# Value weights loaded first, and the last tokens' values of seven blocks computed in the start of a recurrent-memory transformer layer

## The chip, the cores and the metric

The kernel runs on one core of a Trainium2 chip. A core has five engines with queues of their own, each taking its instructions in the order in which they were written: PE (matrix products), DVE (vector), ACT (scalar functions and copies), POOL (general) and SP, which here only starts transfers. The metric is the device time of one execution in microseconds (us). Before the change it is 1035.0 us, the median of three runs (1034.61 to 1038.56).

## The reference

A layer with a recurrent memory over 2048 tokens of width 640, then a dense layer. The tokens are cut into 64 segments of 32. Each segment is preceded by eight memory tokens, and the memory of the next segment is the output of the attention at those eight places. So segment s+1 can't start before segment s has its memory.

```python
mem = mem0                                             # 8 x 640
for s in range(n_seg):                                 # 64 segments
    xs = x[:, s * seg_len:(s + 1) * seg_len, :]        # 32 tokens, normalised
    h = jnp.concatenate([mem, xs], axis=1)             # 40 rows
    q, k, v = h @ Wq, h @ Wk, h @ Wv                   # 32 heads of 128 each
    scores = jnp.where(mask, q @ k.T * scale, -1e9)    # all see mem, tokens causal
    o = softmax(scores) @ v
    o = einsum('bhte,hed->btd', o, Wo)
    mem = o[:, :M, :]
    outs.append(o[:, M:, :])
h = x + concatenate(outs)
h2 = h + relu(layernorm(h) @ w1 + b1) ** 2 @ w2 + b2
```

## The kernel before

**Tiling.** Sixteen blocks of four segments; a segment is one step, written (b, sp). Of the 40 rows of a segment, 32 (8 of memory and the first 24 tokens) are projected in the step itself, with four matrix products side by side in the four 32-column strips of PE (`proj`). The last 8 tokens of the four segments of a block, 32 rows together, are projected apart, since they need no memory: `tail_units(b, which)` gives ten units of four matmuls for q, k or v of block b. A unit is small work that can be put anywhere; the list `fill` holds the units waiting, and `run(fill, n)` in a step issues n of them at places where PE would wait: one before the values, two after them, five while the output is summed, the rest while the memory is transposed.

**What a block's fill is.** In block b (from 1 to 14), step sp=0 carries the ten value units of block b+1, sp=1 its q units, sp=2 its k units, and sp=3 ten units of the output product of the last tokens of block b-1. In block 0 all thirty units of block 1 run in step (0,0), and (0,1) to (0,3) carry none.

**Values through DRAM.** The values of the last tokens are wanted in another arrangement than the projection gives. `tail_out` copies a half (n = 0 or 1) into a row buffer (four in rotation, shared with the q and k rows of the steps), `tails_v` writes it to DRAM (`vt_d`, two blocks in rotation) and `tails_v_in` reads it back into `vt4`. Flips of q and k rows, statistics and sums that are to run at the head of a step are put into the list `late`; `mid` and `win` are lists for the norm and the transposes of a coming block.

**The start.** ACT starts the loads of x blocks 0 and 1 and of the first memory, SP the four weight matrices in the order wq, wk, wv, wo (5.2 MB each). `ln_stats`, `ln_norm` and `ln_transpose` prepare a block of 128 rows: statistics on DVE, two small operations on POOL (L151, L152), the norm on DVE, five transposes on PE, and two copies on ACT, one to `hT4` (first 24 tokens of each segment, L180) and one to `hTt` (last 8, L181). `start()` then projects segment 0 and the last tokens of block 0 chunk by chunk, as the weights come: q, k, v. After it, `tails_in` brings the q and k of the last tokens to their place (POOL), and step (0,0) begins with scores. In this step POOL issues the four reads of block 0's values.

**Semaphores of transfers.** Transfers started by SP and ACT share eight semaphores in turn, and a transfer is started only once the one before it on the same semaphore has landed.

Of the kernel before, what the change touches and what calls it, by code (L numbers as in the profile page):

```python
# [9 lines left out]
ALU = mybir.AluOpType  # L10
# [6 lines left out]
def kernel(  # L17
# [16 lines left out]
    nc = tc.nc  # L34
# [83 lines left out]
    def load_x(b, eng=nc.sync):  # L118
        xt = s2.tile([128, D], BF16, tag="xt", name="xt")
        eng.dma_start(out=xt[:], in_=x2d[b * 128:(b + 1) * 128, :])  # L120
        xts[b] = xt

    load_x(0, nc.scalar)
    load_x(1, nc.scalar)
    o_ring = [const.tile([128, DH], BF16, name="o%d" % k) for k in range(5)]
    for o in o_ring:
        nc.gpsimd.memset(o[64:128], 0.0)
# [2 lines left out]
    for ch in range(2):  # L130
        nc.scalar.dma_start(out=o0[32 * ch:32 * ch + M, :].rearrange("m (c f) -> m c f", f=64),
                            in_=A_mem0[0].rearrange("m (c t f) -> t m c f", t=2, f=64)[ch])
    load_w(wq, A_Wq)
    load_w(wk, A_Wk)
    load_w(wv, A_Wv)
    wov = A_Wo.rearrange("h e d -> e h d")
    for n in range(2):
        for j in range(2):
# [30 lines left out]
    def ln_transpose(b):  # L169

        xn = xns.pop(b)
        pt = mm.tile([128, 1024], BF16, tag="mm", name="pt")
        for c in range(DC):
            nc.tensor.transpose(out=pt[:, c * 128:(c + 1) * 128], in_=xn[:, c * 128:(c + 1) * 128], identity=ident[:])

        def out():
            hT4 = s2.tile([128, DC, 4, SEG], BF16, tag="hT4", name="hT4")
            hTt = s2.tile([128, DC, TL, 4], BF16, tag="hTt", name="hTt")
            ptv = pt[:, 0:640].rearrange("p (c s t) -> p c s t", c=DC, s=4)
            nc.scalar.copy(out=hT4[:, :, :, M:SEG], in_=ptv[:, :, :, 0:HD])  # L180
            nc.scalar.copy(out=hTt[:].rearrange("p c k s -> p c s k"), in_=ptv[:, :, :, HD:SEG])  # L181
            hT4s[b], hTts[b] = hT4, hTt
        return out

    def proj(w, by, lhs, n, ps, c0, c1):
# [20 lines left out]
    def rowtile():  # L206
        return s2.tile([128, 512], BF16, tag="row", name="row", bufs=4)

    def evac_row(which, row, ps):
        if which == "q":  # L210
            nc.scalar.mul(out=row[:], in_=ps, mul=scale)  # L211
        else:
            nc.scalar.copy(out=row[:], in_=ps)  # L213

    def flip(row, dst, n):
        nc.vector.transpose(out=dst[:, n * 16:(n + 1) * 16, 0:32], in_=row[:].rearrange("p (h e) -> p h e", e=32))  # L216

    wov2 = wo[:].rearrange("p h (c t f) -> p h t c f", t=2, f=64)

# [10 lines left out]
    def wo_out(pw):  # L230
        o = o_ring[0]
        o_ring.append(o_ring.pop(0))
        tmp = s1.tile([64, DH], F32, tag="otmp", name="otmp")
        nc.scalar.copy(out=tmp[:], in_=pw[64:128, 0:DH])  # L234
        nc.vector.tensor_tensor(out=o[0:64], in0=pw[0:64, 0:DH], in1=tmp[:], op=ALU.add)  # L235
        return o

    fill, late, mid, win = [], [], [], []
# [1 line left out]
    def run(q, n):  # L240
        while n > 0 and q:
            q.pop(0)()
            n -= 1

    def tail_units(b, which):
        w = {"q": wq, "k": wk, "v": wv}[which]
        lhs = lambda c: hTts[b][:, c].rearrange("p k s -> p (k s)")
# [12 lines left out]
    def tail_out(b, which, n, ps):  # L260
        row = rowtile()
        evac_row(which, row, ps)
        if which == "v":
            tails_v(b, n, row)
            return
        if n == 0:
            tails.setdefault(b, {})[which] = s2.tile([128, H, 32], BF16, tag=which + "Tt", name=which + "Tt")
        dst = tails[b][which]
        late.append(lambda: flip(row, dst, n))
# [32 lines left out]
                              in_=k.unsqueeze(2).to_broadcast([128, H, 4, TL]))  # L302

    vt4s = {}
    vt_d = dram.tile([2, 4, 128, 2 * E], BF16)

    def tails_v(b, n, row):

        eng = nc.scalar if b < 2 else nc.sync
        eng.dma_start(out=vt_d[b % 2, 2 * n:2 * n + 2].rearrange("j r f -> r j f"),  # L310
                      in_=row[:].rearrange("r (j f) -> r j f", j=2))
        if n == 0:
            return
        vt4s[b] = s2.tile([128, 4, 2, E], BF16, tag="vt4", name="vt4")
        if b:
            tails_v_in(b, nc.sync)

    def tails_v_in(b, eng):
        src = vt_d[b % 2].rearrange("j (g k s) f -> g j k (s f)", g=G, s=4)
        for g in range(G):  # L320
            eng.dma_start(out=vt4s[b][32 * g:32 * g + 32].rearrange("p s u e -> p (s u e)"), in_=src[g])

# [31 lines left out]
    def step(b, sp, v=None):  # L354
# [1 line left out]
        last = s == NS - 1  # L356
        hT4 = hT4s[b]
        lhs = lambda c: hT4[:, c, sp, :]
        vt4 = vt4s[b]
# [3 lines left out]
        run(late, 3)  # L363

        def project(which, w, dst, n, between=None):
            if ready:
                if between:
                    between()
                return
            ps = mmtile()  # L370
            proj(w, "columns", lhs, n, ps, 0, DC)
            row = rowtile()
            if not between:
                evac_row(which, row, ps[:])
                flip(row, dst, n)
# [214 lines left out]
    ck, cv = Carve(wk), Carve(wv)  # L590
    f1T = ck(FC * NT).rearrange("p (c t) -> p c t", c=FC)
    hnT0 = const.tile([128, DC, NT], BF16, name="hnT0")
    hnTs = [hnT0[:], ck(DC * NT).rearrange("p (c t) -> p c t", c=DC)]
    ht0 = [const.tile([128, D], BF16, name="ht0%d" % k) for k in range(NK4)]
    ots = [ck(D) for _ in range(4)]
    fxs = [ck(D) for _ in range(4)]
    hbs = [cv(D, F32) for _ in range(2 * NK4)]
# [48 lines left out]
    def start():  # L646

        v = s2.tile([128, EG], BF16, tag="v", name="v")
        tail = lambda c: hTts[0][:, c].rearrange("p k s -> p (k s)")
        main = lambda c: hT4s[0][:, c, 0, :]  # L650
        for which, w, dst in (("q", wq, qT), ("k", wk, kT), ("v", wv, None)):
            pa = pop.tile([128, 4, 512], F32, tag="po", name="pa")
            for c in range(DC):
                for n in range(2):
                    proj(w, "half" if which == "v" else "columns", main, n, pa[:, n, :], c, c + 1)
                for n in range(2):
                    proj(w, "order" if which == "v" else "columns", tail, n, pa[:, 2 + n, :], c, c + 1)
            for n in range(2):
                if which == "v":
                    nc.scalar.copy(out=v[:, n * 512:(n + 1) * 512], in_=pa[:, n, :])  # L660
                else:
                    row = rowtile()
# [7 lines left out]
    for b in range(2):  # L670
        ln_stats(b)
        ln_norm(b)
        ln_transpose(b)()
        if b == 0:
            mem_to_hT(o0, hT4s[0], 0)
    v0 = start()
    tails_in(0, 0)
    for b in range(NB):
        for sp in range(4):
            run(soon, 1)  # L680
            if sp == 0 and b + 2 < NB:
                load_x(b + 2)
            if b == 0 and sp == 0:
                fill += tail_units(1, "v") + tail_units(1, "q") + tail_units(1, "k")
            if 0 < b < NB - 1 and sp < 3:
                fill += tail_units(b + 1, "vqk"[sp])
            if sp == 3 and 0 < b < NB - 1:
                fill += wo_tail_units(b - 1)
            if b == NB - 1 and 0 < sp < 3:
# [5 lines left out]
                mid.append(lambda b=b: ln_norm(b + 2))  # L695
            if b + 2 < NB and sp == 3:
                win.append(lambda b=b: ln_transpose(b + 2))
            e = b * 4 + sp - (NS - 7)
            if (b, sp) == (1, 0):
                ffn_biases()  # L700
# [120 lines left out]
```

## Time and profile before

| | |
|---|---|
| median of the runs | 1035.0 us (1034.61 to 1038.56) |
| the profiled execution | 1033.77 us, its span 1032.0 us |
| PE busy | 974.3 us, 94% of the span |
| DVE, ACT, POOL busy | 618.4, 536.8, 309.0 us |
| step 1's first matmul | 67.0 us |
| steps (0,1) to (15,2) | 66.74 to 882.52 us |
| dense layer and end | the rest |
| mean granted PE clock | 0.992 |

The length of a step is read here from one copy of the memory into `hT` (L296) to the next. Over blocks 1 to 14 (105.84 to 841.94) a step takes 13.15 us on average; the shortest take 12.79. The steps with sp=0 of blocks 1 to 14 took 14.06, 13.16, 13.31, 13.13, 12.96, 13.27, 13.07, 12.89, 12.90, 13.04, 13.26, 12.89, 13.20 and 13.38 us.

A page of the profile lists the busy share of each engine in forty slices. The chain of waits follows the last instruction back, at each step to what released it. The timeline lists instructions in order of time, with the idle time before them and what ended it in brackets. A table of stretches gives the busy time of each engine between two times and the granted clock there.

### The profile page before, as it was taken

How to read it: one execution, taken by the hardware profiler on the slowest of the kernel's cores; microseconds unless marked ns; L12 is line 12 of the kernel's file. 1: busy time of each engine (PE TensorE's matmuls, PEld its weight loads, DVE VectorE, ACT ScalarE, POOL GpSimd, SP SyncE). 2: the span in 40 equal slices, each digit the busy share in tenths (PEclk: the TensorE clock that was granted, in tenths of full speed). 3: DMA queues.
4: the chain of work that ended last, by engine and by line, in shares of the span. 5: the costliest groups of instructions: out<-in, count | busy, mean ns of one | idle time of the engine just before them, and what ended most of it. 6: DMA issues, size and time to landing. Idle time of an engine off the chain costs nothing.

```text
span 1032.0 us, 59015 instructions
## 1 busy us (share of the span) xinstructions
PE 974.3 (94%) x26940; PEld 563.6 (55%) x26940; DVE 618.4 (60%) x1724; ACT 536.8 (52%) x1237; POOL 309.0 (30%) x797
## 2 busy tenths in 40 slices
PE   3678999999999999999999999999999998899998
PEld 1245555565556555555555556555556565555565
DVE  2145566666666666666666666666666676566532
ACT  2235555555555555555555555555555555534431
POOL 1023333333333333333323232333233333343210
PEclk9889999999999999999999999999999999999999
DMA  9930101010000000000000000000000110612200
GB/s 378 396 105 5 33 7 32 10 29 13 25 17 27 14 24 18 25 17 26 17 14 27 15 27 15 26 15 27 15 27 8 52 34 7 195 61 66 77 26 26
DMA packets 38538, 50.93 MB, mean 49 GB/s; under 512 B 6097, under 2 KB 34385, under 8 KB 36369
## 3 DMA queue, kind: packets, MB, share of 16 engines
q1 hardware_dynamic: 36496, 46.04, 13.5%
q8 instruction: 210, 3.44, 1.4%
q10 hardware_dynamic: 1472, 0.86, 0.3%
q0 software_dynamic: 320, 0.26, 0.1%
q14 instruction: 40, 0.32, 0.1%
HBM read 37.71 MB, written 9.44 MB: 46 GB/s over the span
## 4 chain that ended last, share of the span: by engine, by line
PE 86%; DMA 6%; DVE 3%; ACT 2%; issue 2%; SPq 0%; POOL 0%; ACTq 0%; DVEq 0%; POOLq 0%
PE ps L195 46%; PE pw L227 15%; PE y L772 6%; PE ps L740 5%; PE ps L227 3%; PE po L431 2%; DMA wv<-in_A_Wv_dram 2%; PE sm L403 2%; PE pm L294 2%; DMA vt_d<-row 1%; PE po L338 1%; DMA wk<-in_A_Wk_dram 1%; PE ps L477 1%; ACT em L412 1%; DMA xt<-in_A_x_dram 1%
## 5 line engine op out<-in xcount | busy, mean ns | idle before, releaser
L195 PEld LDWEIGHTS <-hT 128*32 128x32 bf16 x7680 | 187.7, 96 | 184.9 <-DVE hT L296 19.2
L195 PE MATMUL ps<-wv,hT 128*32 128x512 bf16 x2520 | 169.9, 379 | 0.7 <-ACT v L484 0.7
L227 PE MATMUL pw<-wo,oT 128*32 128x320 bf16 x4224 | 161.9, 302 | 5.0 <-issue 2.1
L195 PE MATMUL ps<-wq,hT 128*32 128x512 bf16 x2520 | 158.2, 380 | 2.4 <-DVE hT L296 2.4
L195 PE MATMUL ps<-wk,hT 128*32 128x512 bf16 x2520 | 157.7, 379 | 0.0
L227 PEld LDWEIGHTS <-oT 128*32 128x32 bf16 x4224 | 110.4, 97 | 53.2 <-DVE oT L202 16.5
L527 POOL TENSOR_TENSOR pkt<-ek,rk 128x64 bf16<-128x64 bf16 x64 | 19.0, 296 | 374.5 <-DVE rk L525 293.8
L211 ACT ACTIVATE row<-ps 128x512 bf16<-128x512 f32 x156 | 91.9, 600 | 73.1 <-PE ps L195 69.6
L216 DVE STREAM_TRANSPOSE qT<-row 128x512 bf16<-128x512 bf16 x128 | 90.7, 709 | 60.7 <-ACT row L211 60.2
L213 ACT CAST row<-ps 128x512 bf16<-128x512 f32 x123 | 69.9, 597 | 34.0 <-PE ps L195 32.3
L301 POOL COPY kT<-kTt 128x1024 bf16<-128x1024 bf16 x64 | 70.9, 1108 | 7.6 <-DVE kTt L216 7.6
L389 POOL COPY qz<-qT 128x96 bf16<-128x96 bf16 x126 | 33.6, 267 | 126.5 <-DVE qT L216 120.7
L235 DVE TENSOR_TENSOR o<-pw,otmp 64x320 bf16<-64x320 f32 x66 | 31.8, 482 | 63.5 <-ACT otmp L234 63.5
L348 ACT CAST oT<-po 128x512 bf16<-128x512 f32 x128 | 68.7, 589 | 1.6
L195 PEld LDWEIGHTS <-hTt 128*32 128x32 bf16 x1920 | 49.7, 98 | 29.0 <-issue 6.4
L234 ACT COPY otmp<-pw 64x320 f32<-64x320 f32 x66 | 27.9, 422 | 69.8 <-PE pw L227 69.6
L216 DVE STREAM_TRANSPOSE kT<-row 128x512 bf16<-128x512 bf16 x65 | 46.1, 710 | 26.7 <-ACT row L213 26.7
L772 PE MATMUL y<-wq,wk 128*128 128x320 bf16 x416 | 61.1, 299 | 0.2 <-DVE wk L749 0.2
L378 ACT CAST row<-ps 128x256 bf16<-128x256 f32 x126 | 40.7, 375 | 28.4 <-PE ps L195 28.3
L523 DVE TENSOR_REDUCE zk<-ek 128x8 f32<-128x320 bf16 x64 | 31.1, 486 | 38.2 <-ACT ek L519 38.2
L519 ACT ACTIVATE ek<-tk 128x320 bf16<-128x320 f32 x64 | 30.1, 470 | 44.9 <-DVE tk L517 44.9
L484 ACT CAST v<-ps 128x512 bf16<-128x512 f32 x63 | 36.9, 586 | 29.3 <-PE ps L195 29.2
(112 smaller groups left out, 1643.2 us busy)
## 6 DMA issues: line engine op xcount, KB each, us to landing
wq<-in_A_Wq_dram SPq DMA_DIRECT2D x5, 1024.0 KB
wk<-in_A_Wk_dram SPq DMA_DIRECT2D x5, 1024.0 KB
wv<-in_A_Wv_dram SPq DMA_DIRECT2D x5, 1024.0 KB
wo<-in_A_Wo_dram SPq DMA_DIRECT2D x4, 1280.0 KB
vt<-vt_d SPq DMA_DIRECT2D x60, 64.0 KB
vt_d<-row SPq DMA_DIRECT2D x28, 128.0 KB
xt<-in_A_x_dram SPq DMA_DIRECT2D x14, 160.0 KB
wq<-in_B_w_dram SPq DMA_DIRECT2D x1, 2080.0 KB
```

Source lines behind the costliest of these rows:

```text
L195: nc.tensor.matmul(ps[32 * k:32 * k + 32, :], lhsT=lhs(c), rhs=wr[:, c, n, k], start=(c == 0), stop=(c == DC - 1))
L211: nc.scalar.mul(out=row[:], in_=ps, mul=scale)
L213: nc.scalar.copy(out=row[:], in_=ps)
L216: nc.vector.transpose(out=dst[:, n * 16:(n + 1) * 16, 0:32], in_=row[:].rearrange("p (h e) -> p h e", e=32))
L227: nc.tensor.matmul(pw[32 * j:32 * j + 32, 0:DH], lhsT=lhs(p), rhs=wov2[:, head(p), ch], start=(h == 0), stop=(h == 15))
L301: nc.gpsimd.tensor_copy(out=kT[:, :, SEG:2 * SEG].rearrange("p h (j k) -> p h j k", k=TL), in_=k.unsqueeze(2).to_broadcast([128, H, 4, TL]))
L348: nc.scalar.copy(out=oTg[:, n, :, :, M:NK], in_=po[:, :, n * 128:(n + 1) * 128].rearrange("p g (j q) -> p g j q", q=32))
L378: nc.scalar.copy(out=row[:, u * 256:(u + 1) * 256], in_=ps[:, u * 256:(u + 1) * 256])
L389: nc.gpsimd.tensor_copy(out=d.rearrange("p a (j f) -> p a j f", j=3)[:, :, :, 0:M], in_=src[:, :, 0:3, :])
L484: nc.scalar.copy(out=v[:, 0:512], in_=ps0[:])
L740: nc.tensor.matmul(ps[:], lhsT=w1[:, c, fc * 128:(fc + 1) * 128], rhs=hnT[:, c, :], start=(c == 0), stop=(c == DC - 1))
L772: nc.tensor.matmul(y[:, hh, 0:DH], lhsT=f1T[:, fc, k * 128:(k + 1) * 128], rhs=w2[:, fc, cs], start=(fc == 0), stop=False, skip_group_chec ...
```

## The change

1. **Order of weights.** SP loads wv, wq, wk, wo, not wq, wk, wv, wo.
2. **Last rows of four blocks together.** A new `load_tail_rows(g)` loads the 128 last rows of blocks 4g to 4g+3. They are normalised and transposed as a block of their own, keyed `("t", g)`, and one copy gives `hTt` of four blocks. The copy L181 of each block goes. Groups 0 and 1 are prepared in the start, groups 2 and 3 in blocks 2 to 3 and 6 to 7. x block 1 and group 1 are loaded from POOL's queue.
3. **The start.** `start()` projects v first, then q, then k. Behind v it issues the reads of block 0's values on POOL, prepares group 1 and runs the ten value units of block 1. Within stream q run the value units of blocks 2 and 3, within stream k those of block 4 and the q units of block 1, five units behind each of the first four chunks. x block 1 is prepared between streams q and k. The eight value rows of blocks 1 to 4 lie in buffers that the dense layer uses later (`parked`).
4. **Fill.** Step (0,0) carries block 1's k units and the value units of blocks 5 and 6, (0,1) those of block 7. Steps (1,0), (2,0) and (3,0) carry none; from (4,0) to (14,0) the values of blocks 8 to 15 are spread, ten units where b is 4, 6, 8, 10 or 12 and five where it is 5, 7, 9, 11, 13 or 14. The q, k and output units stay where they were.
5. **Values through DRAM.** `vt_d` has a place for every block; SP issues the writes of blocks 1 to 15; the reads of block b+1 are issued at the head of step (b,1).
6. The scratch of `wo_out` shares its buffer with `tk`.

```diff
+    def load_tail_rows(g, eng=nc.sync):
+        xt = s2.tile([128, D], BF16, tag="xt", name="xt")
+        eng.dma_start(out=xt[:], in_=x2d.rearrange("(s t) d -> s t d", t=SEG)[16 * g:16 * g + 16, HD:SEG, :])
+        xts["t", g] = xt
...
-    load_x(1, nc.scalar)
+    load_tail_rows(0, nc.scalar)
...
+    load_w(wv, A_Wv)
     load_w(wq, A_Wq)
     load_w(wk, A_Wk)
-    load_w(wv, A_Wv)
...
         def out():
+            if isinstance(b, tuple):
+                hTt = s2.tile([128, DC, 4, TL, 4], BF16, tag="hTt", name="hTt")
+                nc.scalar.copy(out=hTt[:].rearrange("p c b k s -> p (c b) s k"),
+                               in_=pt[:, 0:640].rearrange("p (a s k) -> p a s k", s=4, k=TL))
+                hTts[b[1]] = hTt
+                return
...
-            nc.scalar.copy(out=hTt[:].rearrange("p c k s -> p c s k"), in_=ptv[:, :, :, HD:SEG])
...
     def tail_out(b, which, n, ps):
-        row = rowtile()
+        row = parked.pop(0) if which == "v" and 0 < b and parked else rowtile()[:]
         evac_row(which, row, ps)
         if which == "v":
-            tails_v(b, n, row)
+            eng = nc.sync if b else nc.scalar
+            eng.dma_start(out=vt_d[b, 2 * n:2 * n + 2].rearrange("j r f -> r j f"),
+                          in_=row.rearrange("r (j f) -> r j f", j=2))
             return
...
         run(late, 3)
+        if sp == 1 and b + 1 < NB:
+            tails_v_in(b + 1, nc.sync)
...
-        if ready:
-            tails_v_in(0, nc.gpsimd)
...
-        run(fill, 100 if ready else 1)
+        run(fill, 10 if ready else 1)
...
-        run(fill, 2)
+        run(fill, 100 if ready else 2)
...
+                if c < DC - 1:
+                    run(units, DC)
...
+        stream("v", wv, None)
+        tails_v_in(0, nc.gpsimd)
+        ln_stats(("t", 1))
+        ln_norm(("t", 1))
+        units += tail_units(1, "v")
+        run(units, 2 * DC)
+        ln_transpose(("t", 1))()
+        units += tail_units(2, "v") + tail_units(3, "v")
+        stream("q", wq, qT)
+        ln_stats(1)
+        ln_norm(1)
+        ln_transpose(1)()
+        units += tail_units(4, "v") + tail_units(1, "q")
+        stream("k", wk, kT)
+        run(late, 100)
...
+    ln_stats(0)
+    ln_norm(0)
+    ln_transpose(0)()
+    load_tail_rows(1, nc.gpsimd)
+    mem_to_hT(o0, hT4s[0], 0)
+    ln_stats(("t", 0))
+    ln_norm(("t", 0))
+    ln_transpose(("t", 0))()
+    load_x(1, nc.gpsimd)
...
             if b == 0 and sp == 0:
-                fill += tail_units(1, "v") + tail_units(1, "q") + tail_units(1, "k")
-            if 0 < b < NB - 1 and sp < 3:
+                fill += tail_units(1, "k") + tail_units(5, "v") + tail_units(6, "v")
+            if b == 0 and sp == 1:
+                fill += tail_units(7, "v")
+            if 0 < b < NB - 1 and 0 < sp < 3:
                 fill += tail_units(b + 1, "vqk"[sp])
+            if b > 3 and sp == 0:
+                for h in halves[:2 if b % 2 == 0 and b < NB - 2 else 1]:
+                    fill += h
+                    halves.remove(h)
```

More of the change, by code (lines that the diff above doesn't have):

```diff
@@ L176, in out @@
         def out():
+            if isinstance(b, tuple):
[4 more added lines that the diff above has]
+                return
             hT4 = s2.tile([128, DC, 4, SEG], BF16, tag="hT4", name="hT4")
-            hTt = s2.tile([128, DC, TL, 4], BF16, tag="hTt", name="hTt")
             ptv = pt[:, 0:640].rearrange("p (c s t) -> p c s t", c=DC, s=4)
             nc.scalar.copy(out=hT4[:, :, :, M:SEG], in_=ptv[:, :, :, 0:HD])
-            nc.scalar.copy(out=hTt[:].rearrange("p c k s -> p c s k"), in_=ptv[:, :, :, HD:SEG])
-            hT4s[b], hTts[b] = hT4, hTt
+            hT4s[b] = hT4
         return out
@@ L210, in evac_row @@
         if which == "q":
-            nc.scalar.mul(out=row[:], in_=ps, mul=scale)
+            nc.scalar.mul(out=row, in_=ps, mul=scale)
         else:
-            nc.scalar.copy(out=row[:], in_=ps)
+            nc.scalar.copy(out=row, in_=ps)
     def flip(row, dst, n):
-        nc.vector.transpose(out=dst[:, n * 16:(n + 1) * 16, 0:32], in_=row[:].rearrange("p (h e) -> p h e", e=32))
+        nc.vector.transpose(out=dst[:, n * 16:(n + 1) * 16, 0:32], in_=row.rearrange("p (h e) -> p h e", e=32))
     wov2 = wo[:].rearrange("p h (c t f) -> p h t c f", t=2, f=64)
@@ L232, in wo_out @@
         o_ring.append(o_ring.pop(0))
-        tmp = s1.tile([64, DH], F32, tag="otmp", name="otmp")
-        nc.scalar.copy(out=tmp[:], in_=pw[64:128, 0:DH])
-        nc.vector.tensor_tensor(out=o[0:64], in0=pw[0:64, 0:DH], in1=tmp[:], op=ALU.add)
+        tmp = s1.tile([128, DH], F32, tag="tk", name="otmp")
+        nc.scalar.copy(out=tmp[0:64], in_=pw[64:128, 0:DH])
+        nc.vector.tensor_tensor(out=o[0:64], in0=pw[0:64, 0:DH], in1=tmp[0:64], op=ALU.add)
         return o
@@ L243, in run, with tail_rows @@
             n -= 1
+    def tail_rows(b, c):
+        return hTts[b // 4][:, c, b % 4].rearrange("p k s -> p (k s)")
     def tail_units(b, which):
         w = {"q": wq, "k": wk, "v": wv}[which]
-        lhs = lambda c: hTts[b][:, c].rearrange("p k s -> p (k s)")
+        lhs = lambda c: tail_rows(b, c)
         st = {}
@@ L304, with tails_v_in @@
     vt4s = {}
[L305 to L313, printed above, removed]
+    vt_d = dram.tile([NB, 4, 128, 2 * E], BF16)
+    def tails_v_in(b, eng):
         vt4s[b] = s2.tile([128, 4, 2, E], BF16, tag="vt4", name="vt4")
[L315 to L319, printed above, removed]
+        src = vt_d[b].rearrange("j (g k s) f -> g j k (s f)", g=G, s=4)
         for g in range(G):
@@ L358, in step @@
         lhs = lambda c: hT4[:, c, sp, :]
-        vt4 = vt4s[b]
         ready = v is not None
@@ L363, in step @@
         run(late, 3)
+        if sp == 1 and b + 1 < NB:
+            tails_v_in(b + 1, nc.sync)
+        vt4 = vt4s[b]
         def project(which, w, dst, n, between=None):
@@ L373, in project @@
             if not between:
-                evac_row(which, row, ps[:])
-                flip(row, dst, n)
+                evac_row(which, row[:], ps[:])
+                flip(row[:], dst, n)
                 return
@@ L592 @@
     hnT0 = const.tile([128, DC, NT], BF16, name="hnT0")
+    ht0 = [const.tile([128, D], BF16, name="ht0%d" % k) for k in range(NK4)]
+    parked = [hnT0[:, c, :] for c in range(DC)] + [ht0[k][:, 0:512] for k in range(3)]
     hnTs = [hnT0[:], ck(DC * NT).rearrange("p (c t) -> p c t", c=DC)]
-    ht0 = [const.tile([128, D], BF16, name="ht0%d" % k) for k in range(NK4)]
     ots = [ck(D) for _ in range(4)]
@@ L648, in start, with stream @@
         v = s2.tile([128, EG], BF16, tag="v", name="v")
-        tail = lambda c: hTts[0][:, c].rearrange("p k s -> p (k s)")
         main = lambda c: hT4s[0][:, c, 0, :]
-        for which, w, dst in (("q", wq, qT), ("k", wk, kT), ("v", wv, None)):
+        units = []
+        def stream(which, w, dst):
             pa = pop.tile([128, 4, 512], F32, tag="po", name="pa")
@@ L656, in start @@
                 for n in range(2):
-                    proj(w, "order" if which == "v" else "columns", tail, n, pa[:, 2 + n, :], c, c + 1)
+                    proj(w, "order" if which == "v" else "columns", lambda c: tail_rows(0, c), n, pa[:, 2 + n, :], c, c + 1)
+                if c < DC - 1:
+                    run(units, DC)
             for n in range(2):
@@ L661, in start @@
                 else:
-                    row = rowtile()
+                    row = rowtile()[:]
                     evac_row(which, row, pa[:, n, :])
@@ L667, in start @@
             run(late, 100)
-        return v
[L670 to L675, printed above, removed]
+        stream("v", wv, None)
[13 more added lines that the diff above has]
+        run(late, 100)
+        return v
+    ln_stats(0)
[7 more added lines that the diff above has]
+    load_x(1, nc.gpsimd)
     v0 = start()
     tails_in(0, 0)
+    halves = [h for b in range(8, NB) for h in (tail_units(b, "v")[:DC], tail_units(b, "v")[DC:])]
     for b in range(NB):
@@ L697 @@
                 win.append(lambda b=b: ln_transpose(b + 2))
+            if b in (2, 6) and sp == 1:
+                load_tail_rows(b // 4 + 2)
+                tg = ("t", b // 4 + 2)
+            if b in (2, 6) and sp == 3:
+                late.append(lambda tg=tg: ln_stats(tg))
+                mid.append(lambda tg=tg: ln_norm(tg))
+            if b in (3, 7) and sp == 0:
+                win.append(lambda tg=tg: ln_transpose(tg))
             e = b * 4 + sp - (NS - 7)
```

## The prediction

> **What bounds the kernel now.** I read the page's slices first, then the chain of waits in order of time for the first 110 us, the timeline of POOL and DVE there, and last the busy time of each engine step by step.
>
> ```profile
> PE   3678999999999999999999999999999998899998
> PEclk9889999999999999999999999999999999999999
> DMA  9930101010000000000000000000000110612200
> ```
>
> One digit is 25.8 us. The DMA engines are full for two slices (weights), PE is part idle for four, then PE is busy to the end. So two stages have different limits: a start fed by transfers, and 63 steps.
>
> ```profile
> 9.39 12.38 DMA wk<-in_A_Wk_dram
> 21.79 21.15 DMA wv<-in_A_Wv_dram
> ...
> 46.72 7.33 DMA vt_d<-row
> 54.09 0.67 issue
> 54.77 0.83 POOL vt L321
> 55.59 4.07 DMA vt<-vt_d
> ...
> 60.87 4.49 PE pw L227 x63
> ...
> 67.00 4.50 PE ps L195 x80
> ...
> 76.18 2.39 PE pw L227 x64
> ```
>
> The chain (start, length, what): the last weights, wv, arrive at 42.9; block 0's last-token values go out to DRAM (7.33) and come back (4.07); step 1 starts at 67.0. The same 64 matmuls of L227 take 4.49 us at 60.9 and 2.39 at 76.2: the clock.
>
> ```profile
> 54.77 2.56 POOL L321 DMA_DIRECT2D vt<-vt_d  x4 [18.23 <-DMA vt_d<-row]
> 63.15 0.30 POOL L527 TENSOR_TENSOR pkt<-ek,rk 128x64 bf16<-128x64 bf16 x1 [5.82 <-DVE rk L525]
> ```
>
> POOL, in order of time. It takes no instruction while its read of the values waits for their write: 18.23 us of idle time, then 2.56 us for the four read issues. Here nothing stood behind it that was wanted before 63.
>
> ```profile
> 48.80:52.20 3.40, 3.40 (x40) 1.62 (x36) 0.65 (x3) 1.23 (x3) 0.00 (x0) 0.50 1.09 375
> 52.20:59.00 6.80, 4.20 (x92) 2.25 (x84) 2.73 (x4) 2.27 (x4) 2.56 (x4) 1.00 0.92 311
> 59.00:65.80 6.80, 5.40 (x88) 2.87 (x88) 1.87 (x5) 1.16 (x3) 2.26 (x4) 0.50 0.13 44
> ```
> ```profile
> 80.01:92.93 12.92, 10.79 (x360) 6.39 (x360) 7.81 (x24) 6.55 (x17) 4.12 (x11) 1.00 0.02 4
> 172.78:185.61 12.83, 12.83 (x408) 7.31 (x400) 8.42 (x25) 7.56 (x19) 4.64 (x13) 1.00 0.17 48
> 211.51:224.82 13.31, 13.20 (x416) 8.10 (x406) 7.97 (x23) 6.96 (x18) 3.93 (x11) 1.00 0.08 21
> ```
>
> Stretches: length, busy PE, PEld, DVE, ACT, POOL (instructions), granted clock, DMA. First three: the clock is 0.50 from 48.8 and 59.0, after PE stood idle 44.4 to 47.6 and 56.4 to 59.1, and is full again 4.3 us after work resumed at 47.85 and 5.0 us after 60.87. Last three are whole steps: (0,2) with no filling work takes 12.92 us with PE busy 10.79; (2,1) with ten fill units takes 12.83 with PE never idle. **Ten units, 2.16 us of PE, lengthen a step by nothing**: they lie in the waits of the recurrence (softmax 1.56 us between the last scores and the values, then 1.07 us from the output matmuls to the transposed memory).
>
> **The change part by part.** A group of four matmuls (one unit) costs 0.216 us at full clock (80 in 4.32 us at 211.99) and 0.43 at half (group starts 17.04, 17.47, 17.89).
>
> *Fill taken out of steps.* 30 units leave (1,0) to (3,0), 30 more leave the sp=0 steps of blocks 5, 7, 9, 11, 13 and 14 (five each); (0,1) gains ten. At 0.216 the net 50 units would be 10.8 us. By the step rows it is nearly nothing: bare steps took 13.27, 12.92, 12.91. Blocks 2 and 3 go from 13.16 and 13.31 to about 12.95: 0.6. Step (1,0), 14.06 with a bias load that holds POOL, keeps most: 0.2. The six half-filled ones sum to 78.77 and go to about 6 x 12.95 = 77.7: 1.1. Row buffers held by a value write delayed one following step, (11,1), by 1.0; half such writes remain: 0.3. Sum -2.2; bounds +2 (two wider ACT copies, new waits) and -13 (60 units in full). I take the value near the rows of bare steps.
>
> *Last rows normalised apart.* 16 copies of L181 (0.51) go, four of 640 columns come (estimate 0.75, from 0.56 for 480 and 0.59 for 512), with four more loads, statistics, norms and five transposes (0.4 to 0.7 us of PE) each. Groups 2 and 3 fall in bare or half-filled steps: nothing. Groups 0 and 1 are on the path. The scratch tile shared with tk adds no wait: ACT and DVE keep the order already.
>
> *The start.* Order on PE becomes: values of block 0, ten units of block 1's values, transposes of group 1's rows, stream q with 20 units, transposes of x block 1, stream k with 20 units, step 0.
> 1. The first stream keeps its place: 16.63 to 23.5 now for wq; 23.7 with the wider copy.
> 2. ACT copies v and rows and issues the second write of block 0's values: 2.69 us after the stream's end today (44.03 to 46.72), so 26.4.
> 3. On POOL, the four reads of these values come *before* the two L151/L152 operations of group 1. So they wait until the write lands. Price of the landing: 3.56 us for such a write in a quiet step (644.67), 7.33 in the start beside 1280-byte pieces, and longer beside weights: in the first 8 us 1280-byte pieces and 8192-byte pieces of the two queues ended one for one, 41 to 47 each per us. 512 pieces then take 11 to 12 us after some 3.5 us of latency. SP's fourth wk chunk waits for the first of these writes (one semaphore), so weights run dry near 37 and the tail gets quicker. Ends 30.0 and 42; I take 39, because eight-KB traffic is what runs there.
> 4. POOL: 2.56 + 0.25 + 0.57 + gaps = 3.5; DVE norm 0.45; transposes 0.72: 43.8. PE's ten units ended at 25.9. **PE stands 17 us**, and DVE and ACT behind it too: q's flips and evictions queue there.
> 5. Stream q: 40 groups, the clock cold. 4.7 us at half clock are 11 groups, 29 x 0.216 = 6.3: 11.0, so 54.8.
> 6. x block 1: its statistics stand on DVE behind four flips. From the stream's end: ACT row 0.65, flips to 3.5, statistics 1.1, POOL 0.95, norm 0.5, PE starts 6.15 later and transposes 0.45: 61.4.
> 7. Stream k: wk has landed (45 to 46, a chunk each 2.5 us), clock cold again after 6 us idle: 11.0, so 72.4.
> 8. Now k is last, so its rows are not hidden: two evictions, four flips with block 1's q ahead of the tail's, POOL's 1.1 us copy and qz: 6.5 us to the scores, which today follow at once. Then scores to fill 1.7, ten cold units 4.3, values 0.9, twenty units 4.3, output 2.4, memory 1.65, and small gaps: 21.7. Step 1 starts at 94.1, not 67.0: **+27.1**. The early values do save the 3 us wait at 56 to 59, and that is inside the count.
>
> The Trainium skill (TensorE: Matmul & The Clock Gate, Part 1) has the clock back after about 3.4 us of sustained work; the rows say 4.3 to 5.0. By the page each of the three cold starts would cost 1.7 us and not 2.35, and the sum would be 2 us less. The skill (DMA: Bandwidth & Descriptors, Anatomy of one DMA) gives 2.0 us plus bytes over 436 GB/s, 2.3 us for a 131 KB write; the row shows 7.33. By the page POOL would be held 10 us less and step 1 start near 84.
>
> **Sum.** 27.1 - 2.2 = 24.9. The profiled execution took 1033.77 (span 1032.0) and becomes 1058.7; the median shown, 1035.0, is 1.2 above it: 1060.
>
> **Rivals.**
> A. *POOL is not held* (not slower). If the statistics are served before the read, or the write has landed by 22.4 (25.9 less 3.5), the 17 us are gone: stream q 26.4 to 35.1, x block 1 to 41.7, k to 50.4 at full clock, step 1 at 72.1: +5.1 - 2.2, 1038 (1040 with a cold k). For: POOL is idle 17 us before. Against: the order of the instructions and the 18.23 us row; a write issued at 26.4 can't land at 22.
> B. *The write lands early*, at 30.0 as in quiet steps: 9 us less, 1051. Against: full DMA engines there.
> C. *Steps follow their matmuls*: 13 us given back instead of 2.2: 1049. For: PE 100% busy in filled steps. Against: the bare steps of 12.92.
> D. *Landing at 42, and all cold stretches 6.8 us long* (the longest half-clock window seen): +3 and 3 x 1.05: 1066.
>
> **How the numbers follow.** Forecast 0.68, A 0.09, B 0.09, C 0.07, D 0.07. The likeliest gives 1060; its neighbours B, C and D set 1046 to 1067, a little below C since B and C can both hold in part. A is left out. A measurement of this kernel tells about 0.5% (5 us) from no change: slower 0.88, within 0.07 (A), faster 0.05 (A together with C).
>
> **What would show it.** Right: POOL's reads of block 0's values waiting over 8 us right after the first stream, L151 behind them, PE idle from 26 to about 43 with the transposes released by the DVE norm, half clock in streams q and k, step 1 near 94, sp=0 steps of 12.9 to 13.2. Wrong: PE busy from 16 to 45, or steps falling to 11.

## The result, and the profile after

The changed kernel takes 1064.48 us in the median of four runs (1062.79 to 1067.19), the kernel before 1036.37 in four runs (the three of the section on time, and one more; 1034.61 to 1038.56). The ratio is 1.0273, with a 95% interval of 1.0240 to 1.0305: slower. The profiled execution has a span of 1060.3 us, against 1032.0 before, 28.3 more. The memory of step 0 is copied to `hT` at 93.80, before at 66.74 (+27.06). From there to the last copy the 62 steps take 816.87, before 815.78 (+1.1). The dense layer takes 149.7, before 149.5. So the loss is the start.

The page's slices, busy PE, granted clock and DMA (one digit is 26.5 us now):

```profile
PE   4359889998999999999999999999999998899998
PEclk9689999999999999999999999999999999999999
DMA  9941010100010101000101010101000110522200
```

In the second and third slice, 26.5 to 79.5, PE is at 3 and 5 tenths, where the kernel before had 6 and 7, and the clock is at 6 and 8 tenths. From the fourth slice on PE is at 8 or 9 as before.

The chain of waits of the first 100 us (start, length, what):

```profile
18.51 6.37 PE pa L205 x70
24.93 0.46 issue
25.39 0.59 ACT v L670
25.98 0.50 ACT row L223
26.50 9.39 DMA vt_d<-row
35.90 5.07 DMA wk<-in_A_Wk_dram
40.97 2.35 POOL vt L327 x4
43.35 0.25 POOL lnrs L157
43.67 0.58 POOL lnrs L158
44.28 0.46 DVE xn L171
44.78 0.71 PE pt L180 x5
...
56.76 0.61 ACT row L221
...
62.46 0.71 PE pt L180 x5
...
74.14 0.59 ACT row L223
...
78.49 1.08 POOL kT L316
```

It is read as a sentence. Block 0's values are written from 26.50 on; the four reads on POOL start only at 40.97; behind them stand the two small operations of the last rows' statistics (`lnrs`); behind these the norm (`xn`) and the transposes (`pt`), and only then can stream q start. The first matmul of step 1 is at 94.06; the prediction had 94.1.

The timeline of POOL, with the idle time before an instruction and its releaser in brackets:

```profile
16.38 0.66 POOL L120 DMA_DIRECT2D xt<-in_A_x_dram  x1 [0.79 <-DVE xn L171]
40.95 2.37 POOL L327 DMA_DIRECT2D vt<-vt_d  x4 [23.91 <-DMA wk<-in_A_Wk_dram]
43.35 0.24 POOL L157 TENSOR_SCALAR lnrs<-lnmv 128x1 f32<-128x1 f32 x1
43.67 0.57 POOL L158 TENSOR_TENSOR lnrs<-lnrs,mhalf 128x1 f32<-128x1 f32 x1
```

POOL took nothing for 23.91 us. The profile names a weight chunk as the releaser, because transfers share semaphores; but SP's fifth wk chunk, which waited for the second value write, went out at 40.29, so this write had just landed, and in an experiment below the same wait ends at 40.76 and is put down to the value write. The statistics that L157 works on had been ready since 17.1 (DVE's L155: 0.21 us from 16.90).

The timeline of PE, where it stood:

```profile
44.78 0.71 PE L180 MATMUL pt<-ident,xn 128*128 128x128 bf16 x5 [17.78 <-DVE xn L171]
62.46 0.71 PE L180 MATMUL pt<-ident,xn 128*128 128x128 bf16 x5 [5.75 <-DVE xn L171]
79.84 0.41 PE L411 MATMUL sm<-kT,qz 128*32 128x64 bf16 x16 [5.75 <-POOL qz L397]
```

Three waits, 29.3 us. What they make of the clock is in the table of stretches (length, busy PE, PEld, DVE, ACT, POOL with instructions, granted clock, DMA share, GB/s):

```profile
25.00:44.78 19.78, 2.00 (x40) 0.71 (x29) 0.45 (x1) 3.12 (x6) 3.18 (x6) 0.63 0.97 384
44.78:56.70 11.92, 11.92 (x165) 5.05 (x165) 0.00 (x0) 3.92 (x5) 0.00 (x0) 0.76 1.07 342
62.46:74.08 11.62, 11.62 (x169) 5.09 (x169) 0.00 (x0) 2.92 (x5) 0.00 (x0) 0.78 0.19 55
74.08:94.06 19.98, 12.38 (x321) 7.11 (x317) 9.23 (x24) 7.52 (x17) 3.74 (x9) 0.83 0.11 30
```

Streams q and k are busy from end to end, but run at a mean clock of 0.76 and 0.78: each wait is paid a second time. The records of the clock have it at half from 29.98 to 50.46, from 60.70 to 67.52 and from 77.76 to 84.59. These stretches are 6, 2 and 2 times 3.41 us long. The Trainium skill (TensorE: Matmul & The Clock Gate, Part 1) says that the clock is decided in free-running windows of about 3.4 us; the lengths here agree. After PE's work resumed (44.78, 62.46, 79.84) the half clock lasted 5.7, 5.1 and 4.8 us, so a cold start cost no fixed time from the first matmul. All three are longer than the 3.4 us of sustained work that the prediction takes from the same page; the measurement decides.

SP stood too. Its queue's waits, first 100 us (total, times, longest):

```profile
SPq L114 <- DMA vt_d<-row: 16.3, 2, 12.3
```

The last two chunks of wk went out at 35.90 and 40.29, once the first and the second value write had landed.

### The profile page after: what moved, and what is told of

The parts are those of the page before. It is cut to its first block, busy times and chain, and to the rows that moved or that the text cites. A ratio compares the mean times of both kernels' runs of the same rounds, so it can differ in the third digit from the quotient of the medians.

```text
span 1060.3 us, 58908 instructions
## 1 busy us (share of the span) xinstructions
PE 979.0 (92%) x26960; PEld 564.8 (53%) x26960; DVE 623.3 (59%) x1740; ACT 536.5 (51%) x1225; POOL 313.5 (30%) x807
## 3 DMA queue, kind: packets, MB, share of 16 engines
q1 hardware_dynamic: 37328, 46.63, 13.5%
## 4 chain that ended last, share of the span: by engine, by line
PE 84%; DVE 6%; DMA 5%; ACT 3%; issue 2%; POOL 1%; SPq 0%; ACTq 0%; DVEq 0%; POOLq 0%
PE ps L205 46%; PE pw L237 13%; PE y L816 5%; PE ps L784 4%; PE ps L237 3%; PE po L439 2%; PE pm L309 2%; PE pa L205 2%; PE sm L411 2%; DMA wq<-in_B_w_dram 1%; DMA vt_d<-row 1%; PE po L344 1%; PE ps L483 1%; DMA o<-in_A_mem_dram 1%; ACT em L420 1%
## 5 line engine op out<-in xcount | busy, mean ns | idle before, releaser
L223 ACT CAST row<-ps 128x512 bf16<-128x512 f32 x115 | 66.0, 595 | 34.4 <-PE ps L205 34.3
L244 ACT COPY otmp<-pw 64x320 f32<-64x320 f32 x66 | 27.9, 422 | 72.2 <-PE pw L237 72.2
L420 ACT ACTIVATE em<-sm,mx 128x64 bf16<-128x64 f32 x126 | 40.4, 321 | 23.7 <-DVE mx L417 23.7
```

Of the source, the lines that this page charges most:

```text
L223: nc.scalar.copy(out=row, in_=ps)
L420: nc.scalar.activation(out=em[:], in_=sms[n][:, 0:2 * SEG], func=ACT.Exp, bias=mx[:, 0:1], scale=1.0, accum_out=zm[:])
```

## The experiments

All are kernels made from the changed one unless it says "before". "Kernel 7" is the kernel of experiment 7. The time of step 1 is the copy of step 0's memory to `hT` (before 66.74, after 93.80); "the steps" are the time from there to the last such copy (815.78 and 816.87).

**1. Reads of the values behind the statistics of the last rows.**

```diff
         stream("v", wv, None)
-        tails_v_in(0, nc.gpsimd)
         ln_stats(("t", 1))
         ln_norm(("t", 1))
+        tails_v_in(0, nc.gpsimd)
```

> The changed kernel, with the four POOL reads of block 0's values issued behind group 1's statistics and norm. Theory (POOL held by the read): the 17.8 us for which PE waits for group 1's norm go; stream q runs from about 27 to 36; but x block 1's two POOL operations still stand behind the read, which lands near 40 and ends its issues near 43.4, so stream k starts near 45.5 and step 1 near 76: about 1047. Rival 1 (the transfers are what binds: SP's last wk chunk waits for the write of these values): stream k ends no earlier than now, 74, and the time stays near 1064. Rival 2 (steps follow their matmuls) says nothing of it.

Measured: 1044.75 us (one run; before 1035.89 in the runs on that chip), step 1 at 75.62, the steps 817.29. Its POOL timeline:

```profile
17.34 0.22 POOL L157 TENSOR_SCALAR lnrs<-lnmv 128x1 f32<-128x1 f32 x1 [0.17 <-DVE lnmv L155]
...
40.76 2.43 POOL L327 DMA_DIRECT2D vt<-vt_d  x4 [22.55 <-DMA vt_d<-row]
43.22 0.24 POOL L157 TENSOR_SCALAR lnrs<-lnmv 128x1 f32<-128x1 f32 x1
```

The wait on POOL is nearly as long as in the changed kernel (22.55 and 23.91), yet 18.2 us of the loss are gone: only what stood behind the wait counted. The L157 at 43.22 is that of x block 1, which now stands behind the reads; PE still waits 8.7 us for it.

**2. Reads behind x block 1 too.** The line `tails_v_in(0, nc.gpsimd)` goes behind `ln_norm(1)`, after stream q.

> The same, with the reads behind x block 1's norm too. Theory: POOL holds nobody; stream k starts about 6.5 us after stream q's end, near 42.5, cold, ends near 53.5, step 1 near 73.5: about 1044. Rival 1 (transfers bind): near 1064, or no better than with the reads behind group 1 alone.

Measured: 1043.83 (one run), step 1 at 73.95, the steps 818.80. The reads start last, at 43.75, but x block 1's L157 still came only at 42.83, after 24.37 us of idle time released by DVE: DVE had its statistics queued behind q's flips, and these waited for a row buffer that holds block 0's values until their write lands. The write has a second hold.

**3. All statistics first.** Statistics and norm of the last rows and the statistics of x block 1 stand before stream v, the norm of x block 1 before stream q, its transposes behind stream q.

```diff
+        ln_stats(("t", 1))
+        ln_norm(("t", 1))
+        ln_stats(1)
         stream("v", wv, None)
         tails_v_in(0, nc.gpsimd)
-        ln_stats(("t", 1))
-        ln_norm(("t", 1))
...
+        ln_norm(1)
         stream("q", wq, qT)
-        ln_stats(1)
-        ln_norm(1)
         ln_transpose(1)()
```

> Statistics of group 1 and of x block 1 ahead of stream v, x block 1's norm ahead of stream q, the reads behind them. Theory: only the two evictions (2 us) stand between streams q and k, the last wk chunk (held by the write of block 0's values, landing near 45) is the next limit, k ends near 46 to 48, step 1 near 66 to 68: 1036 to 1039, no change against before. Rival (the early units save step time that the start hid): faster than before by the 50 units, 10.8 us, so near 1026.

Measured: 1041.74 (10 runs, 1039.02 to 1042.99), ratio to before 1.0046 (1.0032 to 1.0059), step 1 at 72.11, the steps 818.38. The two waits for norms are gone, and the expectation was still missed, by 3 to 6 us. ACT's timeline shows by what:

```profile
36.13 1.57 ACT L221 ACTIVATE row<-pa 128x512 bf16<-128x512 f32 x3 [0.28 <-PE pa L205]
40.01 0.60 ACT L221 ACTIVATE row<-pa 128x512 bf16<-128x512 f32 x1 [2.31 <-DMA vt_d<-row]
```

The second row of q's last tokens waits for the row buffer with block 0's values until 40.01; stream k needs the accumulators that this row frees and starts cold (half clock 39.26 to 46.08). PE's timeline:

```profile
40.66 1.05 PE L205 MATMUL pa<-wk,hT 128*32 128x512 bf16 x8 [4.20 <-ACT row L221]
```

It is the hold that experiment 2 had shown on DVE, and the rule "put the read last" doesn't reach it.

**4. Is the fill in the steps worth anything?** The kernel *before*, with the value units of blocks 2 to 15 left out; 140 units of four matmuls are not computed, and those blocks use block 1's values.

```diff
-            if 0 < b < NB - 1 and sp < 3:
+            if 0 < b < NB - 1 and 0 < sp < 3:
                 fill += tail_units(b + 1, "vqk"[sp])
+            if 0 < b < NB - 1 and sp == 0:
+                vt4s[b + 1] = vt4s[1]
```

> The kernel before, with the value units of blocks 2 to 15 left out (140 units; these blocks use block 1's values for their last tokens). Theory (fill lies in waits): the bare sp=0 steps take 12.9 to 13.0, sp=1 steps lose their row waits; 1031 to 1037. Rival (steps follow their matmuls): 140 x 0.216 = 30 us less, near 1006.

Measured: 1036.4 (one run; before 1035.89), the steps 814.65, 1.1 less. The sp=0 steps of blocks 1 to 14 take 12.99 on average instead of 13.18, which is 2.7 in all; the other steps give most of it back. At 0.216 us a unit it would have been 30 us. This kernel's dense layer took 153.1 in its profile where the others' took 148.4 to 150.8, which isn't explained, so its steps are the better witness than its time.

**5. and 6. The shared scratch.** The changed kernel with a scratch of its own for the first 67 sums, and the kernel *before* with the shared one. Both were run with the kernel before on one chip.

```diff
-        tmp = s1.tile([128, DH], F32, tag="tk", name="otmp")
+        outs_made.append(o)
+        if len(outs_made) < 68:
+            tmp = ht0[3][:].bitcast(F32)
+        else:
+            tmp = s1.tile([128, DH], F32, tag="tk", name="otmp")[:]
...
```

> The changed kernel, with the sum's scratch in a buffer of its own again (one of the dense layer's, idle until step 60; the last 15 sums keep the shared one). In the changed kernel all 82 copies into the scratch wait for two semaphores, before it 39 of 82, and the copy starts 107 ns after the last matmul where it starts 53 ns after it with one wait. Theory (a second wait on the path costs 0.054 us a step): with about 40 steps at one wait again, some 2 us less than the changed kernel, 1062. Rival (the 0.05 us of every step come from the fill that was taken out): no change, 1064.5.

Measured: 1059.34 (5 runs; before 1034.29 on that chip), ratio 1.0250 (1.0227 to 1.0272); the interval overlaps that of the change itself (1.0240 to 1.0305). The shortest steps are 12.80 again instead of 12.85, the steps 816.21.

```diff
-        tmp = s1.tile([64, DH], F32, tag="otmp", name="otmp")
+        tmp = s1.tile([128, DH], F32, tag="tk", name="otmp")
...
```

> The kernel before with the scratch shared with tk, and nothing else. Theory: 43 copies more with two waits, 43 x 0.054 = 2.3 us more, 1038.5, and the floor of the filled steps goes from 12.80 to 12.85. Rival: no change, 1036.

Measured: 1035.89 (12 runs; before 1034.29), ratio 1.0029 (1.0013 to 1.0045); the shortest filled steps go from 12.80 to 12.85, the steps to 817.24 (+1.5). The wait can be counted. The answers for the line of this copy, of the kernel before:

```profile
L234 ACT COPY otmp<-pw x66: 422/422/425, 65.4 to 904.1; 64x320 f32<-64x320 f32 x66
L234 ACTq EVENT_SEMAPHORE  x39: 17/17/17, 78.6 to 907.5; - x39
...
  PE pw L227: 69.6, 65
```

and of the changed kernel:

```profile
L244 ACTq EVENT_SEMAPHORE  x82: 17/17/17, 92.4 to 936.0; - x82
L244 ACT COPY otmp<-pw x66: 422/422/424, 92.4 to 931.4; 64x320 f32<-64x320 f32 x66
...
  PE pw L237: 72.2, 64
```

All 82 copies carry a semaphore instruction of their own on ACT's queue now, 39 before. ACT's idle time until the last `pw` matmul is 1.13 us a copy (72.2 by 64), before 1.07. In the records the gap from the last matmul to the copy is 53 ns with one wait and 107 ns with two. That holds for the `pw` copies, where the semaphore instruction waits for PE, the last to come. On the 16 copies of `ps` it waits for DVE, which had long come, and the copy itself for PE; 15 of them start about 52 ns after the last matmul in both kernels. So the second wait cost time only where the semaphore instruction had the late one. The `pw` copy is on the path of every step. The bare steps (0,2) and (0,3), at 12.92 before and 12.85 with the shared scratch, show no loss, so the 54 ns don't come to the end of each step.

**7. Both repairs: statistics first, own scratch.**

> Statistics first and the scratch of its own, together. Theory: both add, 2 us below the run with statistics first: 1034 to 1037, at best a hair below before. Rival (the start is bound by wo, which lands near 61, whatever precedes it): as the run with statistics first.

Measured: 1038.34 (12 runs; before 1034.29), ratio 1.0039 (1.0024 to 1.0055), step 1 at 72.40, the steps 815.18. The interval overlaps that of experiment 3, so the scratch is too small to be told by the times of this pair. All profiles together tell more: the four kernels with the change's fill and the shared scratch (the change and experiments 1 to 3) took 816.87, 817.29, 818.80 and 818.38 us in the steps, the two with their own 816.21 and 815.18, 2.1 us less in the mean, though profiles of the first kind differ by up to 1.9. The rival, that wo binds the start, isn't borne out: the output product starts at 68.62 straight behind the last value unit, and PE stands in no wait for wo. With steps 0.6 shorter than before, step 1's 5.7 us of delay is what keeps this kernel behind.

**8. The write off the row buffers and off the shared semaphores.** Kernel 7, with block 0's value rows in parked buffers and their write issued from POOL; block 4's value units move from stream k to step (0,2), since a parked pair goes to block 0.

```diff
-        row = parked.pop(0) if which == "v" and 0 < b and parked else rowtile()[:]
+        row = parked.pop(0) if which == "v" and parked else rowtile()[:]
...
-            eng = nc.sync if b else nc.scalar
+            eng = nc.sync if b else nc.gpsimd
```

> Statistics first and own scratch, and now the write of block 0's values issued by POOL from two of the parked rows (block 4's value units go from stream k to step (0,2), so that eight parked rows are enough). Theory (the slow write also holds SP's wk chunks and two row buffers): no q row waits for the write, stream k starts near 38.5 and not 40.7, the last wk chunk lands near 43 and not 45, stream k ends near 46 to 47 and step 1 starts near 66 to 67: 1033 to 1035. Rival (the row buffer's wait lies beside others): step 1 at 72 as before, 1038.

Measured: 1034.33 (one run; before 1035.28), step 1 at 68.64, the steps 814.77. Stream k starts at 38.38. Its POOL timeline:

```profile
26.84 1.54 POOL L284 DMA_DIRECT2D vt_d<-hnT  x2 [1.86 <-ACT hnT L223]
36.12 2.47 POOL L333 DMA_DIRECT2D vt<-vt_d  x4 [7.74 <-DMA vt_d<-hnT]
```

The write is issued at about the same time as in the change, and the reads start 4.8 us earlier. Both holds are gone; buffer, queue and the move of block 4's units were changed together, so the share of each in the 3.8 us isn't shown. What ends stream k late is now the weights themselves (last chunk at 46.6, PE waits 2.4), with the clock at half from 46.73 to 60.38, and step 1 is later than the 66 to 67 expected.

**9. The start filled better.** Kernel 8 with fill 0 before step 0's values, only block 1's k units in step 0, the rows' flips run inside the streams, and the values of blocks 4 to 7 in steps (0,1), (0,2), (0,3) and (1,0).

```diff
-        run(fill, 10 if ready else 1)
+        run(fill, 0 if ready else 1)
...
+                    run(late, 100)
...
-                fill += tail_units(1, "k") + tail_units(5, "v") + tail_units(6, "v")
-            if b == 0 and sp in (1, 2):
-                fill += tail_units((7, 4)[sp - 1], "v")
+                fill += tail_units(1, "k")
+            if (b, sp) in ((0, 1), (0, 2), (0, 3), (1, 0)):
+                fill += tail_units(b + sp + 3 if b == 0 else 7, "v")
```

> The same, with step (0,0) relieved: the value units of blocks 4 to 7 lie in (0,1), (0,2), (0,3) and (1,0), which are bare otherwise, block 1's k units behind the values while wo lands, and block 1's q flips within stream k. Theory (ten units in a bare step are free; twenty in step (0,0) cost 4.3 us): the output product starts when wo has landed, near 59 to 60, step 1 near 63 to 65, the steps as in the kernel before: 1030 to 1034, at or just below before. Rival (steps follow their matmuls): the 40 units moved cost 8.6 us there, 1038 and more.

Measured: 1036.91 (12 runs), ratio 1.0018 (1.0001 to 1.0034). Step 1 is at 64.78, 2 us earlier than before, and the steps take 819.19: missed. Step (1,0) alone took 17.1 us, before 14.06. POOL's timeline there:

```profile
107.26 0.45 POOL L562 TENSOR_TENSOR pTx<-pTt,same 128x32 bf16<-128x32 bf16 x2
112.12 0.20 POOL L582 CAST b1f<-b1b 128x14 f32<-128x14 bf16 x1 [4.41 <-DMA b1b<-in_B_b_dram]
112.25 0.27 POOL L403 COPY qz<-qT 128x96 bf16<-128x96 bf16 x1
```

It is the mechanism of the start a second time: an instruction for the dense layer, wanted some 780 us later (first use at 897.5 in kernel 10), waits on POOL for its load, and `qz`, wanted by the scores, stands behind it. SP issued the load's parts from 108.20 on, behind block 7's value write (105.96 and 106.45). PE waited 2.5 us for `qz`, and the clock was at half from 112.93 to 116.34.

**10. The bias copied later.** Kernel 9 with the values of blocks 6 and 7 in (2,0) and (3,0), and the copy of b1 in step (2,1) instead of right behind its load.

```diff
-            if (b, sp) in ((0, 1), (0, 2), (0, 3), (1, 0)):
-                fill += tail_units(b + sp + 3 if b == 0 else 7, "v")
+            if (b, sp) in ((0, 1), (0, 2), (2, 0), (3, 0)):
+                fill += tail_units(b + sp + 3 if b == 0 else b + 4, "v")
...
-        nc.gpsimd.tensor_copy(out=b1f[:], in_=b1b[:])
...
+            if (b, sp) == (2, 1):
+                nc.gpsimd.tensor_copy(out=b1f[:], in_=b1b[:])
```

> The kernel "best" with two edits: the value units of blocks 6 and 7 go into steps (2,0) and (3,0) instead of (0,3) and (1,0), and GpSimd's copy of the first bias b1 is issued five steps after its load instead of right behind it. My theory is that in step (1,0) GpSimd stood for the load of b1, which stood on SP's queue behind block 7's value write, and held qz behind it: 17.1 us in "best", 14.06 in the kernel before. By it step (1,0) falls to 12.9 to 13.1, (0,3) to 13.1 to 13.4, step 1 still begins near 64.8, and the steps take 813.5 to 816 in all; the time is 1030 to 1033 where the kernel before has 1035, a ratio of 0.995 to 0.999. The rival, that the last tokens' value writes on SP are themselves what slows the early steps (rows and x loads late), keeps (0,2) at 13.5 and moves the rest of the loss to (2,0) and (3,0), which then exceed 13.6 each: 1035 to 1037 and a ratio of 1.000 to 1.002.

Measured: 1031.49 us (10 runs, 1030.22 to 1032.75; before 1034.49 in 15 runs), ratio 0.9966 (0.9954 to 0.9978): faster than the kernel before by a third of a per cent, and so than the changed kernel. Step (1,0) is 12.91, as expected, and was 14.06 in the kernel before. Two things left this step at once, the copy and block 7's units; in the change and in experiments 1 to 3, 5, 7 and 8, where it has the copy but no fill, it took 13.52 to 14.14, so the copy alone is worth some 0.6 to 1.2 us there; the rest came with block 7's units. Step 1 is at 65.68 and the steps take 816.29, both a little more than expected: (0,2) stayed at 13.42, near the rival's 13.5; (2,0) took 13.03, against the rival; (3,0) took 14.19, above its 13.6. But there the chain of waits shows another holder, ACT:

```profile
220.84 1.51 ACT hTt L185
222.35 0.01 issue
222.36 0.43 ACT ht L250
222.79 0.02 issue
222.82 0.49 DVE o L251
```

The new wide copy to `hTt` takes 1.51 us, and the copy that sums the memory (here into `ht`) stands behind it. Cutting it in parts was not tried. The profiles place 1.1 us of the gain in the start, lose 0.5 in the steps, and have the dense layer 1.1 shorter, which no edit touches; where all of the 3 us sit isn't settled.

## Why the prediction was right, point by point

The forecast was slower, 1060 (1046 to 1067); 1064.48 came. The mechanism was the one that was told, and the rivals with other mechanisms fell.

- *Steps 1 and 2, the first stream and the write.* The stream ended at 24.85, not 23.7: the wide copy to `hTt` was put at 0.75 us and took 1.57, from 16.88, and PE waited 0.7 for it. The second write went out 2.69 us after the stream's end, exactly as in the row of before, at 27.54 instead of 26.4.
- *Step 3, the landing.* 39 was told, bounds 30 and 42. POOL's reads start at 40.95, so the write had landed near 40.2 by the 0.7 us that lay between landing and read before, and by SP's chunk at 40.29. Counted from the transfers' records, 47 to 50 pieces of 8192 bytes and 42 to 68 of 512 bytes ended in each us from 30 to 38: one for one, as the prediction took it. The longer landing is the later write. Rival B (landing at 30, 1051) is out. D's time, 1066, is the nearest to the median, but its prices are not what was found: it had the landing at 42 and 6.8 us of half clock at each cold start, where 5.7, 5.1 and 4.8 us fell on work (4.7 told).
- *Step 4, PE stands 17 us.* It stood 17.78, and experiment 1 shows that the order on POOL was the cause: with the same wait and the statistics ahead of it 18.2 us came back.
- *Steps 5 to 7.* Stream q 11.3 us (11.0 told), x block 1 6.4 (6.6), stream k 11.0 (11.0).
- *Step 8.* 20.0 us from stream k to step 1, 21.7 told: the scores came 5.75 after the stream (6.5), the ten cold units 3.7 (4.3), the values 0.4 (0.9). This 1.7 made up for the 1.6 that steps 1 to 3 were late, so it is luck that +27.1 was hit to the tenth.
- *Rival A (POOL not held, 1038 to 1040)* named the two conditions under which the loss is gone. Experiment 3 meets the first, statistics before the reads, and gave 1041.74. Its step 1 started at 72.36, A's 72.1, but by other parts: A had 6.6 us for the norm of x block 1, which experiment 3 moved away, and lacked the 4.2 us for the row buffer that the write holds. The rest of the difference lies in the steps, 2.6 us longer than before where A had 2.2 shorter.

**The step that failed is the second term, "sum -2.2" for the fill and the scratch.** The steps became 1.1 longer. "Blocks 2 and 3 ... 0.6", "step (1,0) ... 0.2" and "the six half-filled ones ... 1.1" were to come back in sp=0 steps; these went from 184.52 to 184.34 in all, and the full 1.0 that step (11,1) gave back was lost in other steps. The mean of rows of bare steps was the wrong measure: filled and bare steps have nearly the same floor (12.80 to 12.92), and what lies above it in single steps didn't go with the fill: without 140 units experiment 4 has the steps 1.1 shorter. In some of the long steps the chain names a late value write ((11,1) before, (4,1) after) or the bias load ((1,0)); in others, (3,0) before and (6,0) after, it is nearly all PE, and their cause stays open. And "the scratch tile shared with tk adds no wait" was wrong: the order on ACT and DVE was kept already, but the copy must be told so by a second semaphore. By experiment 6 it costs 0.13 to 0.45% as a ratio, 1.5 us in the steps; by experiment 5 its removal gives 0.7 in the steps, and nothing that the times can tell; by all profiles with the same fill it is some 2. With 1.5 for the scratch, the fill gave back 0.4 and not 2.2; a profile each can't tell that from nothing. Rival C (13 us given back) erred on the same side and further.

The span grew by 28.3: 27.1 in the start, 1.1 in the steps and 0.2 in the dense layer, against 24.9 told. The remaining difference to 1064.48 lies in the medians: that of the four runs is 1.7 us above the profiled one (1062.79), where the prediction put 1.2.

## What to carry to other kernels

An instruction that must wait for a transfer held every instruction behind it on its engine (POOL stood 23.91 us for a read in the change, 4.41 for a copy in kernel 9): put all work that others want soon ahead of it. A write out of a rotating buffer holds the buffer, and the shared semaphore holds the next loads, until it lands, so give a small write beside a weight stream a buffer and a queue of its own (kernel 8). Work that lies in the waits of a recurrence costs little there: 30 us of matmuls less made the steps of experiment 4 1.1 us shorter, and in no run here did moving such work to the start shorten the steps by more than some 1.0 us (kernel 8).

## What was not expected of the hardware

- **The size of the pieces went by the queue.** The same value write, 0.26 MB, went from ACT's queue in pieces of 512 bytes and from POOL's in pieces of 4096. The answers on transfers from 26 to 42 of the changed kernel and from 26 to 37 of kernel 8 (packets, MB, share of 16 engines):

```profile
q10 hardware_dynamic: 544, 0.26, 5.5%
```
```profile
q0 software_dynamic: 96, 0.26, 6.2%
```

  Of the 544 and 96 packets 512 and 64 carry the data; the others have 4 bytes. From the issue of the first write to both landed it took 13.7 us on ACT's queue (26.50 to 40.2) and 8.6 on POOL's (26.84 to 35.4, the 36.12 above less 0.7). The Trainium skill (DMA: Bandwidth & Descriptors, Anatomy of one DMA) gives, for a transfer issued on POOL, a fixed 2.0 us and the bytes over 436 GB/s, by which an estimate for both writes together is 2.6 us; beside a stream of weights neither row comes near it. The prediction's row of 7.33 was on ACT's queue, which that section doesn't speak of. The bytes were the same; queue and size of the pieces changed together, so which of the two made the difference isn't shown.
- **A second semaphore took 54 ns on the `pw` copies** (gap 53 and 107 ns), with an instruction of 17 ns on ACT's queue, and nothing on the `ps` copies, where PE's semaphore was the copy's own (52 ns).
- **A copy of 640 columns with its output strided took 1.57 us**, where 480 columns to `hT` took 0.56. The row of 480 columns, scaled by width, gives the 0.75 of the prediction. The nearer row was L181 itself, with an output strided in the same way: 160 columns in 0.51 us. That the stride is the reason wasn't tested.
